# A gMLP and FFT kernel whose opening is dealt out anew among VectorE, ScalarE and GpSimd

## The chip, the cores and the metric

The kernel runs on one core of a Trainium2 chip. The metric is the device time of one execution in microseconds (us). Engines are named as in the profile: PE is TensorE's matmul (PEld its weight load), DVE is VectorE, ACT is ScalarE, POOL is GpSimd, SP is SyncE, which only issues DMAs here.

## The reference, cut to what matters

Two branches work on the same normalized input and are summed with it. The change touches the first half of branch B only, and the normalization ahead of it.

```python
xn = _layernorm(x)                               # x: 2048 x 448
return x + _A_ref(xn, w_r, w_i) + _B_ref(xn, w1, w2, w3, w4)

def _A_ref(x, w_r, w_i):                         # spectral filter
    X = rfft2(x) * (w_r + 1j * w_i)
    return irfft2(X)

def _B_ref(x, w1, w2, w3, w4):
    h = _gelu(_layernorm(x) @ w1)                # 448 x 448
    hs = concatenate(quarters of h, shifted by +1, -1, +2, -2 tokens) @ w2
    x1 = x + hs
    h2 = _gelu(_layernorm(x1) @ w3) @ w4         # 448 x 1792, 1792 x 448
    return x1 + h2
```

## The kernel before

The 2048 tokens are 16 blocks of 128. They are taken in four groups of four blocks: `GRP = [[14, 15, 0, 1], [2, 3, 4, 5], [6, 7, 8, 9], [10, 11, 12, 13]]`; two blocks share one tile `xt`. Every f32 operand of a product is split into a high and a low f16 half, and three products (high times high, high times low, low times high) replace one.

The opening does for each group, in this order: statistics of each block on VectorE (`stats`, `bn_stats` at L306 and `bn_aggr` at L307) and a first inverse root of the variance (L324 to L328); the normalization of each of the four blocks in place (`norm1`, L333 on ScalarE, L336 on VectorE or GpSimd, the engine of each block given by a list); transposes of the four blocks on TensorE (L389, `T1`); their evacuation into the f16 tile `xT`, the high half by ScalarE (L393), the low half by VectorE (L394). Then come the products with w1 (`w1_in`, L420), one unit to a block; gelu (L459) and the scaled high half (L460) on ScalarE, and the low half on VectorE in two pieces (L462). These are written into shifted slots of `x2mem`. A DMA transpose on SP's queue (L470) then makes `h` of a block, once all units that write into its slot are through. `w2_tile` (L478) multiplies an `h` block by the split w2, and L479 adds the result to the block on VectorE, scaled by `cs`. The last group takes another way: ScalarE and VectorE split it into halves (`turn`, L860 to L862) and DMA transposes (L863) turn it.

GpSimd also refines the inverse root in a run of small steps (L343 to L352), which end in `gsc`, the scale for the group's gelu, and makes `cs` for the residual (`scales`, L360 to L367).

The weights are scaled by powers of two taken from their sums of squares: ScalarE squares them (`squares`, L253), VectorE sums (L258), TensorE adds up over the partitions (L260), and VectorE makes the scale (`powers`, L262 to L267). `split_w` then splits a weight. Without an engine named for the low half, ScalarE makes the high half (L280) and VectorE the low one (L281). With GpSimd named, GpSimd first scales the weight in place (L276), ScalarE copies the high half (L277) and GpSimd subtracts (L278). Quarters 0 and 1 of w1 go the first way, 2 and 3 the second, and so do all four of w2. Two DMAs (L924, L925) then copy w2's halves to the other partitions.

The order on each engine's queue is fixed when the program is built: a scheduler sorts the instructions, bound by the written order, by priorities and by `behind(...)`, which puts an engine's instructions behind a named earlier one of that engine. It adds no wait. At run time each engine goes through its queue in order, and so does SP.

Of the kernel before, what the change touches and what calls it, by code (L numbers as in the profile page):

```python
# [125 lines left out]
def body(tc, nc, x, wf, w1, w2, w3, w4, c_g, c_n, c_small, out):  # L126
# [32 lines left out]
    pc = pool("pc")  # L159
# [8 lines left out]
    def xb(b):  # L168
        return xt[b // 2][:, b % 2]
# [103 lines left out]

    def split_w(hi, lo, src, s, low=None):
        if low is P:
            after["ps"] = (P.tensor_scalar(out=src, in0=src, scalar1=s, scalar2=0.0, op0=ALU.mult, op1=ALU.add).ins,)  # L276
            i = A.activation(out=hi, in_=src, func=AF.Copy)  # L277
            j = P.tensor_tensor(out=lo, in0=src, in1=hi, op=ALU.subtract)  # L278
            return i.ins, j.ins
        i = A.activation(out=hi, in_=src, func=AF.Copy, scale=s)  # L280
        j = V.scalar_tensor_tensor(out=lo, in0=src, scalar=s, in1=hi, op0=ALU.mult, op1=ALU.subtract)  # L281
        return i.ins, j.ins
# [16 lines left out]

    def stats(src, key, mv=None, pins=None):  # L300
        if mv is None:
            mv = pc.tile([128, 4, 2], F32, tag="mv", bufs=3, name=f"mv{key}")
        for i, s in enumerate(src):
            st = pc.tile([128, 6], F32, tag="st", bufs=4, name=f"st{key}_{i}")
            with behind(*pins[i]) if pins else contextlib.nullcontext():
                V.bn_stats(out=st, in_=s)  # L306
            V.bn_aggr(out=mv[:, i, :], in_=st)  # L307
        return mv
# [9 lines left out]

    def norm1(g, apply, pins=None):

        bs, c = GRP[g], slice(4 * g, 4 * g + 4)
        mv, a, y, nm = mva[:, c], va[:, :, c], vy[:, :, c], nma[:, c]
        stats([xb(b) for b in bs], f"a{g}", mv, pins)
        V.tensor_scalar(out=a[:, 1], in0=mv[:, :, 1], scalar1=1.0 + EPS, scalar2=EPS * EPS, op0=ALU.mult, op1=ALU.add)  # L324
# [118 lines left out]
    def wrap_on():  # L443
        move(pairs[1], pairs[0], -1)
# [442 lines left out]
    for t in range(2):  # L887
        w1_in(0, list(enumerate(first)), [t])
    n = 2
    for unit in list(enumerate(first))[:n]:  # L890
        w1_in(0, [unit], [2, 3])
# [6 lines left out]
    with behind("T", "a1"):  # L898
        for unit in list(enumerate(first))[n:2]:
            w1_in(0, [unit], [2, 3])  # L900
    with behind("n", 1), behind("u"):
        s2, r2 = powers(m2, 1, "2", first[0][:, 448:512])
    with behind("p2"):
        for unit in list(enumerate(first))[2:]:
            w1_in(0, [unit], [2, 3])
    s12 = pc.tile([128, 4], F32, name="s12")
# [9 lines left out]
    with behind("a1"), behind("n", 2):  # L916
        for k in range(2, 4):
            w1_unit(0, k, first[k])
    wrap_on()
    with behind("g", 1), behind("na", 2):  # L920
# [187 lines left out]
```

## Time and profile before

| what | value |
|---|---|
| time, median of 3 runs | 408.12 us (407.88 to 408.28) |
| the profiled execution | 408.05 us |
| its span | 406.3 us |
| mean granted TensorE clock | 0.998 |
| TensorE busy over the span | 399.9 us, 98% |
| VectorE, ScalarE, GpSimd busy | 82%, 63%, 25% |

The span is the time between the first and the last instruction of the profile; the rest of the execution's time lies around it. Rows of a timeline give the start in us, the duration of the row's instructions together, the engine, the line, the operation, the tile written and those read, the count, and in brackets the idle time ahead of the row and what ended it. A row's duration can reach past the start of the next, since instructions overlap at their ends. A row of a DMA list gives the size and the time from issue to landing.

### The profile page before, as it was taken

How to read it: one execution, taken by the hardware profiler on the slowest of the kernel's cores; microseconds unless marked ns; L12 is line 12 of the kernel's file. 1: busy time of each engine (PE TensorE's matmuls, PEld its weight loads, DVE VectorE, ACT ScalarE, POOL GpSimd, SP SyncE). 2: the span in 40 equal slices, each digit the busy share in tenths (PEclk: the TensorE clock that was granted, in tenths of full speed). 3: DMA queues.
4: the chain of work that ended last, by engine and by line, in shares of the span. 5: the costliest groups of instructions: out<-in, count | busy, mean ns of one | idle time of the engine just before them, and what ended most of it. 6: DMA issues, size and time to landing. Idle time of an engine off the chain costs nothing.

```text
span 406.3 us, 8732 instructions
## 1 busy us (share of the span) xinstructions
PE 399.9 (98%) x3391; PEld 297.2 (73%) x3391; DVE 333.6 (82%) x702; ACT 255.1 (63%) x433; POOL 100.4 (25%) x158
## 2 busy tenths in 40 slices
PE   8999999999999999999999999999999999999996
PEld 3555555865667877777878878777677779998995
DVE  5898799898947887988698888965999999965645
ACT  4788889874568857655698878853354544353431
POOL 6859910111146946500021111110000000000000
PEclk9999999999999999999999999999999999999999
DMA  8978975567489661637256556510011023100101
GB/s 280 389 272 160 249 152 138 122 121 163 95 225 266 234 191 46 219 95 185 72 144 164 162 142 161 139 27 2 24 69 70 24 90 92 47 2 2 45 2 45
DMA packets 54596, 52.07 MB, mean 128 GB/s; under 512 B 35678, under 2 KB 48542, under 8 KB 54556
## 3 DMA queue, kind: packets, MB, share of 16 engines
q1 hardware_dynamic: 54556, 51.53, 46.0%
q8 instruction: 26, 0.43, 0.4%
q14 instruction: 14, 0.11, 0.1%
HBM read 38.28 MB, written 3.67 MB: 103 GB/s over the span
## 4 chain that ended last, share of the span: by engine, by line
PE 87%; POOL 5%; DMA 2%; DVE 2%; ACT 2%; issue 1%; SPq 0%; POOLq 0%; ACTq 0%
PE pw L400 33%; PE acc L808 23%; PE pw L478 6%; PE side L778 4%; PE acc L778 3%; PE pu L667 3%; PE ps L567 3%; PE pe L688 2%; PE pp L622 2%; PE px L639 2%; PE py L709 2%; PE pw L420 2%; DMA w1s<-w 1%; POOL xt L336 1%; DMA h<-x2mem 1%
## 5 line engine op out<-in xcount | busy, mean ns | idle before, releaser
L400 PE MATMUL pw<-x2mem,w3p 128*128 128x256 f16 x1232 | 151.3, 273 | 0.0
L400 PEld LDWEIGHTS <-w3p 128*128 128x128 f16 x1232 | 118.9, 98 | 19.3
L808 PE MATMUL acc<-w4p,hf 128*128 128x448 f16 (+1 forms) x516 | 104.4, 348 | 0.0
L808 PEld LDWEIGHTS <-hf 128*128 128x128 f16 x516 | 50.1, 98 | 37.6
L726 ACT ACTIVATE pw<-pw,pe 128x512 f32<-128x512 f32 x42 | 27.4, 654 | 26.8 <-PE pw L400 26.6
L729 DVE SCALAR_TENSOR_TENSOR hf<-pw,h,hf 128x512 f16<-128x512 f32 x42 | 31.3, 746 | 12.9 <-ACT hf L728 12.7
L478 PE MATMUL pw<-w2p,h 128*128 128x448 f16 x176 | 35.8, 353 | 0.9 <-DMA h<-x2mem 0.9
L420 PE MATMUL pw<-w1p,xT 128*128 128x448 f16 x176 | 34.9, 352 | 0.1
L648 POOL TENSOR_TENSOR z<-te 128x450 f32<-128x450 f32 x16 | 15.7, 983 | 70.8 <-DVE te L646 65.9
L728 ACT ACTIVATE hf<-pw,h 128x512 f16<-128x512 f32 x42 | 28.9, 687 | 5.0 <-PE acc L808 4.0
L478 PEld LDWEIGHTS <-h 128*128 128x128 f16 x176 | 17.0, 98 | 17.0 <-DMA h<-x2mem 2.0
L744 ACT ACTIVATE hz<-g,h 128x896 f16<-128x896 f32 x14 | 14.6, 1044 | 23.1 <-DVE g L741 23.1
L420 PEld LDWEIGHTS <-xT 128*128 128x128 f16 x176 | 17.1, 99 | 16.1 <-DVE xT L394 0.4
L778 PEld LDWEIGHTS <-hz 128*128 128x128 f16 x294 | 28.3, 98 | 0.6
L629 ACT ACTIVATE pf<-pp 64x450 f16<-64x450 f32 x32 | 17.4, 544 | 12.5 <-DVE pf L630 9.7
L630 DVE TENSOR_TENSOR pf<-pp,pf 64x450 f16<-64x450 f32 x32 | 19.9, 622 | 5.1 <-ACT pf L629 4.7
L745 DVE SCALAR_TENSOR_TENSOR hz<-g,h,hz 128x896 f16<-128x896 f32 x14 | 16.1, 1148 | 6.8 <-ACT hz L744 6.8
L550 POOL TENSOR_TENSOR f<-xr 128x452 f32<-128x452 f32 x16 | 19.7, 1251 | 0.6
L558 DVE TENSOR_TENSOR xh<-f,xh 128x452 f16<-128x452 f32 x16 | 14.3, 916 | 5.7 <-ACT xh L557 5.7
L644 ACT ACTIVATE te<-px 64x450 f32<-64x450 f32 x32 | 17.3, 541 | 1.2 <-PE px L639 0.6
L738 ACT ACTIVATE g<-pw,pe 128x512 f32<-128x512 f32 x14 | 9.6, 683 | 11.3 <-PE pw L400 11.3
L547 POOL TENSOR_TENSOR xr<-xf 128x452 f32<-128x452 f32 x8 | 9.2, 1156 | 22.3 <-issue 16.4
(188 smaller groups left out, 705.7 us busy)
## 6 DMA issues: line engine op xcount, KB each, us to landing
wc<-wf SPq DMA_DIRECT2D x32, 225.0 KB, 3.7
wl<-wf SPq DMA_DIRECT2D x8, 450.0 KB, 4.3
xt<-x SPq DMA_DIRECT2D x8, 448.0 KB, 7.1
xf<-x SPq DMA_DIRECT2D x8, 448.0 KB, 4.6
loads<-x SPq DMA_DIRECT2D x7, 448.0 KB, 4.0
out<-xt SPq DMA_DIRECT2D x13, 224.0 KB, 1.9
w3raw<-w SPq DMA_DIRECT2D x3, 896.0 KB, 10.8
gn<-c_g SPq DMA_DIRECT2D x16, 128.0 KB, 3.0
```

The costliest lines, as they stand in the source:

```text
L400: T.matmul(ps_out, wp[:, wi + t, cols], xT[:, xi + t, tok], start=t == 0 and wi + xi == 0, stop=t == 3 and wi == 4)
L420: m = T.matmul(pm[:, :D], xTs[g][:, xi + t, 128 * i:128 * i + 128], w1p[:, wi + t], start=t == 0 and p == 0, stop=t == 3 and p == 2)
L478: T.matmul(pm[:, :D], h[:, k], w2p[:, w], start=n == 0, stop=n == 10)
L550: P.tensor_tensor(out=f[:, :, k:k + 2].rearrange("p b s d -> p s b d"), in0=u[:, :, 0], in1=u[:, :, 1], op=op)
L629: A.activation(out=hi, in_=src, func=AF.Copy)
L630: V.tensor_tensor(out=lo, in0=src, in1=hi, op=ALU.subtract)
L644: A.activation(out=e[64 * h:64 * h + 64], in_=px_[64 - 64 * h:128 - 64 * h, :2 * DF], func=AF.Copy)
L726: A.activation(out=pm, in_=pm, func=AF.Gelu_apprx_tanh, scale=r3)
L728: i = A.activation(out=h[:, 0], in_=pm, func=AF.Copy, scale=h3)
L729: j = V.scalar_tensor_tensor(out=h[:, 1], in0=pm, scalar=h3, in1=h[:, 0], op0=ALU.mult, op1=ALU.subtract)
L778: m = T.matmul(to, h[:, hi, 128 * blk:128 * blk + 128], b[wi], start=new and n == 0, stop=n == 2 and (last if blk in (2, 5, 3, 0) else end ...
L808: m = T.matmul(to, h[:, hi, o:o + 128], w4p[0][:, wi, f, r], start=first and f % 2 == 0 and n == 0, stop=end and f % 2 == 1 and n == 2, sk ...
```

## The change

Five things are changed.

- The first group is normalized by GpSimd, VectorE, VectorE, VectorE and no longer by GpSimd and VectorE in turn.
- The high half of w1's quarter 0 is made by GpSimd (a scaling into f16) in place of ScalarE. The low half stays on VectorE.
- The second group's fourth block gets its statistics from ScalarE: a copy with accumulation for the mean, a square with accumulation, and a small copy for the variance. The order of the other blocks' statistics is shifted, and the squares of w2 come behind ScalarE's statistics.
- w2 is scaled by GpSimd as before; its first quarter's high half is put directly behind the scalings, the second and third stay behind ScalarE's normalization of the third group, and the fourth is a copy on VectorE. All subtractions stay on GpSimd, behind its normalizations.
- The last product of each of the first two units, which needs the last low half of w1, may now stand behind both units' other products.

```diff
-    def split_w(hi, lo, src, s, low=None):
+    def split_w(hi, lo, src, s, low=None, high=None):
...
-        i = A.activation(out=hi, in_=src, func=AF.Copy, scale=s)
+        if high is P:
+            i = P.tensor_scalar(out=hi, in0=src, scalar1=s, scalar2=0.0, op0=ALU.mult, op1=ALU.add)
+        else:
+            i = A.activation(out=hi, in_=src, func=AF.Copy, scale=s)
...
-    def stats(src, key, mv=None, pins=None):
+    def stats(src, key, mv=None, pins=None, on_a=None):
...
+            if i == on_a:
+
+                sq = pc.tile([128, 1], F32, tag="sq", bufs=2, name=f"sq{key}")
+                junk = xr.bitcast(F32)[:, :D]
+                with behind(*pins[i]):
+                    A.activation(out=junk, in_=s, func=AF.Copy, scale=1.0 / D, accum_out=mv[:, i, 0:1])
+                A.activation(out=junk, in_=s, func=AF.Square, scale=-1.0, bias=mv[:, i, 0:1], accum_out=sq)
+                u = A.activation(out=mv[:, i, 1:2], in_=sq, func=AF.Copy, scale=1.0 / D)
+                after["sq"] = (u.ins,)
+                continue
...
-    n1 = [norm1(0, [P,V,P,V])]
+    n1 = [norm1(0, [P, V, V, V])]
...
-            after["w1", t] = split_w(w1p[:, t], w1p[:, 4 + t], w1s[:, t], s1, P if t > 1 else V)
+            after["w1", t] = split_w(w1p[:, t], w1p[:, 4 + t], w1s[:, t], s1, (V, V, P, P)[t], P if t in (0,) else A)
...
-    n1.append(norm1(1, [P, V, A, V], [("r1",), ("a0", 0), ("w1", 0), ("w1", 1)]))
-    with behind("w1", 3):
+    n1.append(norm1(1, [P, V, A, V], [("e1",), ("w1", 0), ("w1", 1), ("a0", 3)], 3))
+    with behind("sq"):
         squares(m2, flat(w2s))
...
+    r = [slice(0, 128)] * 3 + [slice(0, 64)]
+    with behind("g", 1):
+        for k in range(4):
+            i = P.tensor_scalar(out=w2s[r[k], k], in0=w2s[r[k], k], scalar1=s2[r[k]], scalar2=0.0, op0=ALU.mult, op1=ALU.add)
+    with behind("g", 1):
+        u = A.activation(out=w2p[r[0], 0], in_=w2s[r[0], 0], func=AF.Copy)
+    with behind("np", 2):
+        v = P.tensor_tensor(out=w2p[r[0], 7], in0=w2s[r[0], 0], in1=w2p[r[0], 0], op=ALU.subtract)
...
+    with behind("n", 2):
+        u = V.tensor_copy(out=w2p[r[3], 3], in_=w2s[r[3], 3])
+    with behind("np", 2):
+        v = P.tensor_tensor(out=w2p[r[3], 10], in0=w2s[r[3], 3], in1=w2p[r[3], 3], op=ALU.subtract)
...
     with behind("g", 1), behind("na", 2):
-        for k in range(4):
-            r = slice(0, 128 if k < 3 else 64)
-            after["w2", k] = split_w(w2p[r, k], w2p[r, 7 + k], w2s[r, k], s2[r], P)
```

The edits move instructions on the queues, also where the text is not changed. The changed kernel's lines from L284 on are numbered higher: L276 to L278 keep their numbers, L394 becomes L407, L462 becomes L475, L863 becomes L876 and so on.

GpSimd's queue at the first group, before: the normalizations of two blocks, the two scalings of w1, then the small refining steps (`vq`, from the root `vy`).

```order
L336 TENSOR_SCALAR xt_83<-xt_83,vy,nma 128x448
L336 TENSOR_SCALAR xt_76<-xt_76,vy,nma 128x448
L276 TENSOR_SCALAR w1s<-w1s,pe_205 128x448 x2
L343 TENSOR_TENSOR vq_198<-vy 128x8
L344 TENSOR_TENSOR vq_198<-vq_198,va 128x8
```

The same place in the changed kernel:

```order
L349 TENSOR_SCALAR xt_83<-xt_83,vy,nma 128x448
L281 TENSOR_SCALAR w1p<-w1s,pe_205 128x448
L276 TENSOR_SCALAR w1s<-w1s,pe_205 128x448 x2
L356 TENSOR_TENSOR vq_198<-vy 128x8
L357 TENSOR_TENSOR vq_198<-vq_198,va 128x8
```

One normalization has left, and w1's high half stands between the scale `pe` and the scalings. Everything up to the second group's normalization follows in the same order as before, but for the last low half of w1, which stands one small step earlier.

VectorE's queue at the second group's transposes, before: the sum for w2's scale (`pt`), the low halves of unit 1 (`x2mem<-pw_01`), the low half of the first transposed quarter (`xT<-pta`), the next step of w2's scale, the second quarter.

```order
L258 TENSOR_REDUCE pt_351<-m_168 128x1
L462 SCALAR_TENSOR_TENSOR x2mem<-pw_01_210,h_252,x2mem 128x2x112 x2
L394 TENSOR_TENSOR xT_322<-pta_323,xT_322 128x512
L262 TENSOR_SCALAR pt_351<-pw_00_209 128x1
L394 TENSOR_TENSOR xT_322<-pta_330,xT_322 128x512
```

The same place in the changed kernel:

```order
L258 TENSOR_REDUCE pt_352<-m_168 128x1
L407 TENSOR_TENSOR xT_323<-pta_324,xT_323 128x512
L475 SCALAR_TENSOR_TENSOR x2mem<-pw_01_210,h_252,x2mem 128x2x112 x2
L262 TENSOR_SCALAR pt_352<-pw_00_209 128x1
L407 TENSOR_TENSOR xT_323<-pta_331,xT_323 128x512
```

The first transposed quarter has moved ahead of unit 1's low halves, which now stand between it and the rest. ScalarE's queue has the same exchange for the high halves.

SP's queue after the first four h blocks, before: the rest of w3 and six parts of w4, then the transposes of the last group's halves (`xT<-x`) and of the next four h blocks (`h_598`), in turn.

```order
L223 DMA w3raw<-w 64x1792 x2
L238 DMA w4half<-w 128x6x448
L863 DMA_TRANSPOSE xT_720<-x_721 128x7x128
L470 DMA_TRANSPOSE h_598<-x2mem 128x7x128
L863 DMA_TRANSPOSE xT_720<-x_721 128x7x128 x2
L470 DMA_TRANSPOSE h_598<-x2mem 128x7x128
```

The same place in the changed kernel:

```order
L223 DMA w3raw<-w 64x1792 x2
L238 DMA w4half<-w 128x6x448
L876 DMA_TRANSPOSE xT_721<-x_722 128x7x128 x2
L483 DMA_TRANSPOSE h_599<-x2mem 128x7x128
L876 DMA_TRANSPOSE xT_721<-x_722 128x7x128 x2
L483 DMA_TRANSPOSE h_599<-x2mem 128x7x128 x3
```

Two transposes of the last group stand ahead of the first h block now, where there was one. On TensorE the products of the third group's units are dealt differently around the first two `w2_tile`s: between the first product on the first h block and the first on the second stand 23 products (11 with w2, 12 with w1) where there were 17 (11 and 6). And on GpSimd the four normalizations of the last group stand ahead of most of the steps that make `cs`, and no longer behind them.

More of the change, by code (lines that the diff above doesn't have):

```diff
@@ L888, in body @@
         w1_in(0, list(enumerate(first)), [t])
-    n = 2
-    for unit in list(enumerate(first))[:n]:
-        w1_in(0, [unit], [2, 3])
+    units = list(enumerate(first))
+    w1_in(0, [units[0]], [2, 3])
+    w1_in(0, [units[1]], [2, 3])
     with behind("ps"):
         n1[0]()
-    n1.append(norm1(1, [P, V, A, V], [("r1",), ("a0", 0), ("w1", 0), ("w1", 1)]))
-    with behind("w1", 3):
+    n1.append(norm1(1, [P, V, A, V], [("e1",), ("w1", 0), ("w1", 1), ("a0", 3)], 3))
+    with behind("sq"):
         squares(m2, flat(w2s))
     T1(1)
-    with behind("T", "a1"):
-        for unit in list(enumerate(first))[n:2]:
-            w1_in(0, [unit], [2, 3])
     with behind("n", 1), behind("u"):
@@ L903, in body @@
     with behind("p2"):
-        for unit in list(enumerate(first))[2:]:
-            w1_in(0, [unit], [2, 3])
+        w1_in(0, [units[2]], [2, 3])
+    with behind("p2"):
+        w1_in(0, [units[3]], [2, 3])
     s12 = pc.tile([128, 4], F32, name="s12")
```

16 lines of the change are left out of this document (14 added, 2 removed).

## The prediction

> **What bounds the kernel now.** I read the page's busy times first, then a table by stretches of the span, then TensorE's own timeline.
>
> ```profile
> PE 399.9 (98%) x3391; PEld 297.2 (73%) x3391; DVE 333.6 (82%) x702; ACT 255.1 (63%) x433; POOL 100.4 (25%) x158
> ```
> ```profile
> 53.00:190.00 137.00, 137.00 (x1069) 95.67 (x1068) 117.82 (x246) 95.77 (x161) 44.93 (x51) 1.00 0.62 161
> ...
> 192.00:406.00 214.00, 211.01 (x2052) 173.99 (x2050) 171.78 (x321) 118.72 (x200) 15.73 (x16) 1.00 0.25 72
> ```
> In the table the first number after the stretch is its length, the second TensorE's busy time. From 53 to 190 us TensorE never stops, and hardly after it. So whatever TensorE has lost or won when it reaches 53 us stays to the end; no later slack takes it up. The whole change lies ahead of that point.
>
> ```profile
> 9.54 0.38 PE L260 MATMUL pm<-pt,ones 128*128 128x1 f32 x2 [0.37 <-DVE pt L258]
> ...
> 11.72 6.92 PE L420 MATMUL pw<-w1p,xT 128*128 128x448 f16 x34
> 19.30 1.97 PE L389 MATMUL pta<-ident,xt 128*128 128x128 f32 x16 [0.66 <-POOL xt L336]
> 21.10 0.28 PE L260 MATMUL pw<-pt,ones 128*128 128x1 f32 x2
> 21.24 10.37 PE L420 MATMUL pw<-w1p,xT 128*128 128x448 f16 x54
> 31.45 1.91 PE L389 MATMUL pta<-ident,xt 128*128 128x128 f32 x16
> 33.72 1.31 PE L478 MATMUL pw<-w2p,h 128*128 128x448 f16 x6 [0.36 <-DMA h<-x2mem]
> ...
> 36.00 1.11 PE L478 MATMUL pw<-w2p,h 128*128 128x448 f16 x5
> 37.39 2.26 PE L478 MATMUL pw<-w2p,h 128*128 128x448 f16 x11 [0.28 <-DMA h<-x2mem]
> ...
> 46.67 4.33 PE L478 MATMUL pw<-w2p,h 128*128 128x448 f16 x22
> 51.21 1.12 PE L478 MATMUL pw<-w2p,h 128*128 128x448 f16 x5 [0.22 <-DMA h<-x2mem]
> ```
> Here is what there is to win. The 54 products take 10.37 us, 0.19 each; the last one's record runs 0.16 past the moment at which the next could start, so a true pause is the printed idle time plus 0.16. The pauses: 0.8 us before the second group's transposes at 19.30 (waiting for GpSimd's normalization); 0.5 at 33.72, 0.44 at 37.39 and 0.38 at 51.21, all three for a DMA transpose of h. That is 2.1 us together.
>
> **Term A: the second group's transposes (19.30).** They need all four blocks, and GpSimd's comes last.
>
> ```profile
> 10.82 1.25 POOL L276 TENSOR_SCALAR w1s<-w1s,pe 128x448 f32<-128x448 f32 x2 [0.83 <-DMA w1s<-w]
> ...
> 14.07 0.73 POOL L348 TENSOR_TENSOR vz<-vw 128x8 f32<-128x8 f32 x1
> 14.88 0.20 POOL L349 TENSOR_TENSOR vz<-vz,vq 128x8 f32<-128x8 f32 x1
> ...
> 16.45 1.03 POOL L278 TENSOR_TENSOR w1p<-w1s,w1p 128x448 f16<-128x448 f32 x1
> ...
> 18.30 0.94 POOL L336 TENSOR_SCALAR xt<-xt,vy,nma 128x448 f32<-128x448 f32 x1
> ```
> ```profile
> 10.06 0.18 DVE L307 BATCH_NORM_AGGREGATE mva<-sta 128x2 f32<-128x6 f32 x1
> 10.15 0.13 DVE L262 TENSOR_SCALAR pt<-pm 128x1 f32<-128x1 f32 x1
> ...
> 14.09 0.66 DVE L281 SCALAR_TENSOR_TENSOR w1p<-w1s,pe,w1p 128x448 f16<-128x448 f32 x1
> ...
> 16.92 0.58 DVE L324 TENSOR_SCALAR va<-mva 128x4 f32<-128x4 f32 x1
> 17.42 0.16 DVE L325 TENSOR_SCALAR va<-mva 128x4 f32<-128x4 f32 x1
> ...
> 18.22 1.26 DVE L336 TENSOR_SCALAR xt<-xt,vy,nma 128x448 f32<-128x448 f32 x2
> ```
> GpSimd works without a pause from 10.82 to 18.30. Taking one block of the first group off it ahead of that wins nothing, because at 10.82 it waits for the scale of w1. What the change adds is one operation inside this row of work, the first quarter of w1's high half. The f32 scalings cost 1.25 / 2 = 0.62 each; the subtraction, which also writes f16, 1.03. I take 0.62 (one input, like the scalings) and keep 1.0 as the far end. The scale itself comes 0.15 earlier, since a block's statistics no longer stand between TensorE's sum (done 9.54 + 0.38 = 9.92) and the step at 10.15. So GpSimd reaches its block at 18.30 + 0.62 - 0.15 = 18.77.
>
> VectorE, relieved of one block's statistics (0.53 at its spacing) and of waiting, starts the closing steps of the statistics at about 16.2 and its two normalizations at about 17.1, an estimate from the rows above. That helps VectorE and ScalarE, but neither is last. And it moves VectorE's normalizations onto GpSimd's last split and small steps. A step that costs 0.20 alone (14.88) took 0.73 beside VectorE's split (14.09), so an overlap costs GpSimd up to 0.5; I take 0.2. Its block then runs alone, 0.72 for 0.94, which gives 0.22 back. Sum: 0.62 - 0.15 + 0.2 - 0.22 = 0.45, rounded to **+0.5 us**; ends -0.2 (one of the overlaps with the w1 splits missed) and +1.1 (1.0 for the new operation, 0.5 for the overlap).
>
> The Trainium skill, page "SBUF — State Buffer", section on SBUF's two separate sides, says that the port pair shared by VectorE and GpSimd is an exclusive lock, held for a whole instruction. The 0.58 us at 16.92, against 0.16 for its twin, beside GpSimd's split from 16.45 to 17.48, agrees with it. By that rule both normalizations would lock GpSimd out for their whole length, and A would be near its upper end.
>
> ScalarE's two passes and a copy for the fourth block cost about 0.58 + 0.20 twice and 0.2, by its rows on 448 columns:
>
> ```profile
> 16.09 0.20 ACT L253 ACTIVATION_READ_ACCUMULATOR xr<-w2s 128x1 f32 x1
> 18.22 0.76 ACT L333 ACTIVATE xt<-xt,nma,vy 128x448 f32<-128x448 f32 x1 [1.93 <-DVE nma L328]
> ```
> They are hidden by the 1.93 us in which it waited; without that cover they would cost about 1.7. I cost them at nothing.
>
> **Term B: VectorE behind the transposes.** VectorE now evacuates the first transposed quarter before the two low halves of unit 1, and not after them.
>
> ```profile
> 20.24 0.81 DVE L462 SCALAR_TENSOR_TENSOR x2mem<-pw,h,x2mem 128x224 f16<-128x224 f32 x2 [0.70 <-POOL vw L346]
> 20.97 0.68 DVE L394 TENSOR_TENSOR xT<-pta,xT 128x512 f16<-128x512 f32 x1
> ...
> 27.91 0.81 DVE L462 SCALAR_TENSOR_TENSOR x2mem<-pw,h,x2mem 128x224 f16<-128x224 f32 x2 [0.19 <-ACT x2mem L460]
> ```
> Before, the 0.73 us of those two (spacing 20.24 to 20.97) lay in a hole while the transposes ran. Now the quarter starts some 0.3 sooner after the transposes and the two follow: about 0.4 of later work. The 0.19 idle at 27.91 swallows part. The low halves that complete the first h block, its transpose, and so TensorE's pause at 33.72 move by **+0.25** (ends 0 and 0.4).
>
> **Term C: from the first h transpose to 51.21.** Two things here. On TensorE, 23 products instead of 17 now stand between the first and second h blocks: 33.72 + 23 x 0.19 = 38.1, later than the 37.39 at which the second block released TensorE. The pause of 0.44 goes. ScalarE has two copies fewer ahead of the group's evacuation, so the operands are there. But on SP the second transpose for xT now stands ahead of the first h transpose of the next four blocks, which TensorE needs at 51.21.
>
> ```profile
> 37.80 1.22 SPq L223 DMA_DIRECT2D w3raw<-w  x2
> 39.07 0.59 SPq L238 DMA_DIRECT2D w4half<-w  x1
> 44.65 1.82 SPq L863 DMA_TRANSPOSE xT<-x  x1
> 46.57 1.83 SPq L470 DMA_TRANSPOSE h<-x2mem  x1
> ```
> ```profile
> w4half<-w SPq DMA_DIRECT2D x1, 1344.0 KB, 10.6
> ...
> xT<-x SPq DMA_TRANSPOSE x1, 5.8
> ...
> h<-x2mem SPq DMA_TRANSPOSE x1, 4.6
> xT<-x SPq DMA_TRANSPOSE x1, 3.5
> ```
> The second fence gives the time from issue to landing of each (the last for the one issued at 48.51). The w4 load lands at 39.07 + 10.6 = 49.6, the transposes at 44.65 + 5.8 = 50.4, 46.57 + 4.6 = 51.2 and 48.51 + 3.5 = 52.0. They come out in the order of issue, the first just behind the load and the others 0.8 apart, whatever the issue time. So the transposes queue behind the load. Issuing them about a microsecond earlier, which the changed order on GpSimd and ScalarE allows, wins nothing; one more ahead costs 0.8: the h block lands at 52.0. Slightly earlier loads may give 0 to 0.4 back; I take 0.1. **C = +0.7** for the arrival at 53 us, and it includes the 0.44 just won, since TensorE only waits longer at this gate. GpSimd's scales for the first h block also come some 0.5 to 1.0 later, behind the last group's normalizations, which may stop TensorE at 46.7; the gate swallows that too.
>
> The w2 edits otherwise move cover, not the path: GpSimd's scalings stay where they were, one copy goes to VectorE, and the subtractions end within about 0.2 of before.
>
> **Sum.** 0.5 + 0.25 + 0.7 = 1.45 us on the profiled execution, 408.05 (span 406.3 and 1.75 around it), which stands 0.07 under the median of 408.12: **409.5 us**.
>
> **Rivals.**
> 1. *No extra transpose at the gate.* The h block still lands where it did, because the load ends 0.8 sooner. Then C is 0 and the sum 0.75: 408.8. For it: the load's issue stands behind three h transposes that may flow more smoothly. Against: the 0.8 spacing. Chance 0.15.
> 2. *The lock at full length.* VectorE's two normalizations (1.26 us as they ran) block GpSimd wholly: A = 1.1 and the sum about 2.1, 410.1. It is the rule named above; the 0.73 against 0.20 speaks for it, the 0.94 against 0.72 where they overlapped in full speaks against. Chance 0.13.
> 3. *Faster: the transposes do not queue behind the load.* The mechanism is the gate at 51.21. If h lands by issue time (46.57 + about 3), both 0.44 and 0.38 vanish, C = -0.8, and with A and B near zero the time is 407.2. It decides once the h block lands before 50.4 in the old clock. Against it: 5.8, 4.6 and 3.5, which shrink as the load drains. Chance 0.07.
> 4. *All terms at their small ends*: A 0, B 0, C 0.4, 408.5. Chance 0.07.
>
> **How the numbers follow.** The forecast has 0.58. About 0.2% (0.8 us) is what a measurement here can tell from no change, so slower means over 408.9 and faster under 407.3. Slower: the forecast and rival 2, 0.71, say 0.70. Within: rivals 1 and 4, 0.22. Faster: 0.08. The range runs from the ends near A -0.2, B 0, C 0.3 (408.2) to A 1.1, B 0.4, C 0.8 (410.4).
>
> **What would show it.** A: the second group's transposes start near 19.8, released by GpSimd, with VectorE's normalizations done by about 18. If they start before 19.3, A is wrong. B: the first w2 products come about 2.5 to 2.8 after those of the third group's transposes begin, against 33.72 - 31.45 = 2.27 before. C: no pause before the second h block; one of a microsecond or more before the fifth, released by a DMA transpose that lands 0.8 after the one ahead of it and 2.4 after the w4 load. If that load lands well before 49.6 or the transposes pass it, C is wrong and with it the sign.

## The result, and the profile after

The changed kernel takes 410.18 us (median of 4 runs, 409.88 to 410.42) against 408.00 of the kernel before beside it (407.84 to 408.28): a ratio of 1.0049, 95% interval 1.0037 to 1.0061. It is slower by 2.1 us. Ratios here and below are of fast runs; a single execution of the w2 edits alone that took 1493.08 us is in none of them. The forecast was 409.5, the range 408.2 to 410.4. The profiled execution took 410.19 us with a span of 408.3, 2.0 more than before.

TensorE's timeline of the changed kernel, the rows that answer to those of before (start and duration in us, idle time and its releaser in brackets; 0.16 is to be added to the idle time for the true pause, as in the prediction):

```profile
9.81 0.34 PE L260 MATMUL pm<-pt,ones 128*128 128x1 f32 x2
...
11.79 6.59 PE L433 MATMUL pw<-w1p,xT 128*128 128x448 f16 x34
19.57 1.97 PE L402 MATMUL pta<-ident,xt 128*128 128x128 f32 x16 [1.18 <-POOL xt L349]
...
31.73 1.47 PE L402 MATMUL pta<-ident,xt 128*128 128x128 f32 x12
33.56 0.63 PE L402 MATMUL pta<-ident,xt 128*64 128x128 f32 x4 [0.36 <-DVE x2mem L475]
34.43 1.12 PE L491 MATMUL pw<-w2p,h 128*128 128x448 f16 x5 [0.24 <-DMA h<-x2mem]
...
38.79 2.25 PE L491 MATMUL pw<-w2p,h 128*128 128x448 f16 x11
...
47.87 4.32 PE L491 MATMUL pw<-w2p,h 128*128 128x448 f16 x22 [0.78 <-DVE xt L492]
52.55 2.25 PE L491 MATMUL pw<-w2p,h 128*128 128x448 f16 x11 [0.36 <-DMA h<-x2mem]
...
146.38 0.83 PE L580 MATMUL ps<-csm,xh 128*128 128x128 f16 x12 [0.49 <-DVE y L585]
```

Of the old pauses, the one of 0.5 us ahead of the first w2 product is now two, 0.52 inside the third group's transposes (33.56) and 0.40 behind them (34.43); the second h block (38.79) no longer waits. That at the second group's transposes reads longer (1.18 for 0.66 idle), but only because TensorE has fewer small pauses ahead of it. New are 0.94 at 47.87, where VectorE's addition frees a bank for TensorE's results late, and 0.65 at 146.38, long after the front. Set beside the rows of before, the delay grows at these places:

| TensorE begins | before | after | late by |
|---|---|---|---|
| the sum for w1's scale | 9.54 | 9.81 | 0.27 |
| the second group's transposes | 19.30 | 19.57 | 0.27 |
| the third group's transposes | 31.45 | 31.73 | 0.28 |
| the first w2 product | 33.72 | 34.43 | 0.71 |
| the products of the fifth h block | 51.21 | 52.55 | 1.34 |
| the first FFT product | 131.64 | 133.03 | 1.39 |
| end of the span | 406.3 | 408.3 | 2.0 |

So there are four losses: 0.27 ahead of everything, nothing at the second group's transposes, 0.43 up to the first w2 product, 0.63 up to the fifth h block, and 0.6 after the first FFT product. The table by stretches confirms the last one (the length, then TensorE's busy time): it never stops from 54 to 143 us and then loses half a microsecond.

```profile
54.00:143.00 89.00, 89.00 (x630) 59.28 (x628) 75.27 (x183) 62.95 (x106) 25.46 (x34) 1.00 0.71 165
143.00:148.00 5.00, 4.50 (x45) 3.26 (x44) 4.75 (x6) 2.89 (x6) 4.92 (x4) 1.00 0.39 112
```

In the prediction's terms the profiled execution gives: the opening 0.27 for 0, A 0.0 for 0.5, B 0.43 for 0.25, C 0.63 for 0.7, and about 0.65 that no term covers.

### The profile page after: what moved, and what is told of

Read it like the earlier page. It is cut to its first block, busy times and chain, and to the rows that moved or that the text cites. A ratio compares the mean times of both kernels' runs of the same rounds, so it can differ in the third digit from the quotient of the medians.

```text
span 408.3 us, 8740 instructions
## 1 busy us (share of the span) xinstructions
PE 400.4 (98%) x3391; PEld 297.6 (73%) x3391; DVE 334.3 (82%) x702; ACT 255.1 (62%) x436; POOL 100.1 (25%) x158
## 4 chain that ended last, share of the span: by engine, by line
PE 63%; ACT 3%; POOL 1%; DVE 1%; issue 1%; POOLq 0%
PE pw L413 25%; PE acc L821 17%; PE side L791 4%; PE acc L791 3%; PE pu L680 3%; PE pe L701 2%; PE pp L635 2%; PE px L652 2%; PE py L722 2%; PE ps L580 2%; POOL f L563 1%; ACT xf L554 1%; ACT xh L570 1%; ACT pw L739 1%; ACT hf L741 0%
## 5 line engine op out<-in xcount | busy, mean ns | idle before, releaser
L742 DVE SCALAR_TENSOR_TENSOR hf<-pw,h,hf 128x512 f16<-128x512 f32 x42 | 31.2, 744 | 13.8 <-ACT hf L741 13.5
L491 PEld LDWEIGHTS <-h 128*128 128x128 f16 x176 | 17.1, 98 | 17.1 <-DMA h<-x2mem 1.3
L570 ACT ACTIVATE xh<-f 128x452 f16<-128x452 f32 x16 | 8.7, 573 | 10.6 <-POOL f L563 8.9
```

Of the source, the lines that this page charges most:

```text
L491: T.matmul(pm[:, :D], h[:, k], w2p[:, w], start=n == 0, stop=n == 10)
L742: j = V.scalar_tensor_tensor(out=h[:, 1], in0=pm, scalar=h3, in1=h[:, 0], op0=ALU.mult, op1=ALU.subtract)
```

## The experiments

Theory: B is VectorE's order at the second group's transposes; C is the order of the transposes behind the w4 load; the last 0.65 us come from the changed order on ScalarE and VectorE near 100 us, which delays the fold ahead of the FFT (sums and differences that GpSimd makes of the FFT's input, `xr` and `f`). Rivals: everything is lost at the front; the copy of w2 on VectorE, held up by GpSimd, is the cause of B; the late pause has nothing to do with order. Runs of one front differ in where the sum for w1's scale begins: 9.35, 9.54, 10.08 and 10.14 us in four profiled executions whose code is that of the kernel before up to there, by when the first loads land. So places are compared from that sum, or from the second group's transposes on. The kernel before took 408.0 to 408.1 beside each group of runs.

**The w2 copy back on ScalarE.**

```diff
-    with behind("n", 2):
-        u = V.tensor_copy(out=w2p[r[3], 3], in_=w2s[r[3], 3])
+    with behind("na", 2):
+        u = A.activation(out=w2p[r[3], 3], in_=w2s[r[3], 3], func=AF.Copy)
```

> The changed kernel, with the last quarter of w2's high half copied by ScalarE again and no longer by VectorE. My theory: that copy lasted 1.18 us on VectorE, because GpSimd's subtraction of w2 beside it held it up, and it pushed the low halves of the second group; so without it the new pause of 0.53 us inside the third group's transposes goes, and the first h block lands about 0.4 us sooner against the third group's transposes. How much of that reaches the end depends on GpSimd's scales cs (pause of 0.94 us at 46.7): if they come as before, that pause grows by what was won. I expect 0.4 to 1.0 us less than the changed kernel's 410.2: 409.2 to 409.8. Rival (the copy is only cover, as the prediction had it): the pause inside the transposes stays and the time is 410.2.

409.26 us (409.12 to 409.44, 6 runs), ratio 1.0031 (1.0019 to 1.0042). First the row in question, in the changed kernel, on VectorE and on GpSimd:

```profile
31.61 1.18 DVE L951 CAST w2p<-w2s 64x448 f16<-64x448 f32 x1
```
```profile
31.51 1.03 POOL L938 TENSOR_TENSOR w2p<-w2s,w2p 128x448 f16<-128x448 f32 x1
```

The copy begins 0.10 after the subtraction and ends 0.25 after it. The rule of the Trainium skill, page "SBUF — State Buffer", section on its two separate sides, by which the engine that comes second is blocked for the whole instruction of the first, agrees. TensorE without that copy:

```profile
31.97 1.91 PE L402 MATMUL pta<-ident,xt 128*128 128x128 f32 x16
34.66 1.31 PE L491 MATMUL pw<-w2p,h 128*128 128x448 f16 x6 [0.78 <-DMA h<-x2mem]
```

The pause inside the transposes is gone, and the first w2 product comes no sooner: 2.69 us after the start of these transposes, 2.70 with the copy. The wait for the h block is simply whole again (0.78 + 0.16 for 0.52 + 0.40). So the copy is not the cause of B. The 0.9 us that the run did win came later, with an order of GpSimd's small steps that the edit changed too: GpSimd's scales were ready before TensorE needed the third bank, and no pause stood in the FFT. A pause of 0.67 stayed at the fifth h block (52.26), now released by VectorE's addition. The time was as expected, the reason was not.

**The first group dealt out as before.**

```diff
-    n1 = [norm1(0, [P, V, V, V])]
+    n1 = [norm1(0, [P, V, P, V])]
```

> The changed kernel with the first group's normalizations dealt out as in the kernel before (GpSimd, VectorE, GpSimd, VectorE); one instruction changes its engine and no other moves. My theory: VectorE's third normalization ended late (0.75 us beside GpSimd's), so the sum for w1's scale and the first group's transposes came 0.22 us later; undoing it brings the first transposes from 10.01 back to 9.79, the second group's from 19.57 to about 19.35, and the end about 0.2 us forward: 410.0. Rival (the prediction: taking the block off GpSimd costs nothing): first transposes unchanged against the changed kernel, 410.2. A third possibility: GpSimd is late with its two blocks, and then the second group's transposes do not come earlier.

409.89 us (409.73 to 410.66), ratio 1.0049 (1.0036 to 1.0063): not to be told from the changed kernel. The profiled execution was granted a clock of 0.71 from 10 to 12 us and 0.50 up to 13.4, so it isn't read past the opening. Up to there it shows that GpSimd is through with its two blocks at 10.47, 0.35 before the scale is there, so the third possibility is out. The traces of the changed kernel tell more. VectorE, and what ScalarE had done by then:

```profile
8.05 1.60 DVE L349 TENSOR_SCALAR xt<-xt,vy,nma 128x448 f32<-128x448 f32 x3
9.57 0.14 DVE L258 TENSOR_REDUCE pt<-m 128x1 f32<-128x4 f32 x1
```
```profile
8.79 0.18 ACT L253 ACTIVATION_READ_ACCUMULATOR xr<-w1s 64x1 f32 x1
```

The sum of the squares could have begun at 8.97 and began at 9.57, behind VectorE's third normalization. In another execution of the same front the sum began at 9.33, 0.03 after the last square, since there the weights had landed later. So that normalization costs 0 to 0.57, an estimate from these two executions, by when the loads land. Its mean cost wasn't measured.

**The fifth h block ahead on SP.**

```diff
-            d = SY.dma_start_transpose(out=xTs[g][:, :, 128 * i:128 * i + 128], in_=h)
+            with behind("h", 2, 0) if i else contextlib.nullcontext():
+                d = SY.dma_start_transpose(out=xTs[g][:, :, 128 * i:128 * i + 128], in_=h)
```

> The changed kernel with the DMA transpose of the fifth h block put on SP's queue ahead of the second one for xT; the other engines' queues stay, but for some products on TensorE that trade places. My theory (term C): the transposes come out in the order of issue, 0.77 us apart, behind the w4 load; so the h block lands about 0.77 us sooner, near 51.7, the pause of 0.52 us at 51.84 goes, and the time falls by 0.5 to 409.7. Rival: the order on the queue does not matter, the block lands near 52.5, and the time stays 410.2.

410.19 us (410.02 to 410.96), ratio 1.0057 (1.0045 to 1.0070): no gain at all, though the gate, the wait ahead of the fifth h block, opened as expected. TensorE there and at the FFT:

```profile
47.65 6.49 PE L491 MATMUL pw<-w2p,h 128*128 128x448 f16 x33 [0.80 <-DVE xt L492]
```
```profile
144.96 0.83 PE L580 MATMUL ps<-csm,xh 128*128 128x128 f16 x12 [0.16 <-DVE y L585]
146.37 0.83 PE L580 MATMUL ps<-csm,xh 128*128 128x128 f16 x12 [0.58 <-DVE y L585]
```

33 products stand in one piece: no pause at 51.8. The step of the FFT that waits begins at 146.37, where it began in the changed kernel (146.38). What the front won, a wait 95 us later took back. But the fold had begun 0.42 us sooner (119.87 for 120.29). It lost that in its second part, on GpSimd beside VectorE, whose addition had waited for a load:

```profile
126.98 1.15 DVE L533 SCALAR_TENSOR_TENSOR xt<-xt,s,loads 128x896 f32<-128x896 f32 x1 [0.55 <-DMA loads<-x]
```
```profile
127.71 1.35 POOL L560 TENSOR_TENSOR xr<-xf 128x452 f32<-128x452 f32 x1 [3.76 <-issue]
129.01 1.93 POOL L561 TENSOR_TENSOR xr<-xf 128x452 f32<-128x452 f32 x1
```

In the changed kernel these two steps took 1.06 each, from 128.13; the third part begins at 133.03 in both. So the locally right term was worth nothing in this order. The late wait is not a fixed bound: here it is a sooner start and longer steps. That the other executions lost the gain in the same way isn't shown.

**The last mean subtractions on GpSimd.**

```diff
-    ln2(range(12, 16), [P, A, P, A], ("f", 0, 6))
+    ln2(range(12, 16), [P, P, P, P], ("f", 0, 6))
```

> The changed kernel with the four mean subtractions of the last four blocks of the second normalization all on GpSimd, where two were on ScalarE; nothing else moves. My theory: the last 0.66 us were lost at 145.7, where TensorE waited for the folded input of the FFT, because VectorE gave the last blocks' statistics 3 us later than before, and ScalarE's in-order queue held the gelu behind its mean subtractions. Without those on ScalarE the gelu at 115 comes 1 to 3 us sooner, the fold follows, the pause of 0.66 us goes or shrinks to under 0.2, and the time is 409.5 to 409.8. Rival (all is lost at the front and the pause at 145.7 has another cause): 410.2, with the pause as it was.

410.29 us, ratio 1.0059 (1.0046 to 1.0071). The pause at 145 shrank only from 0.66 to 0.52. ScalarE's gelu did come 3.0 us sooner (112.11 for 115.07), but then ScalarE waited:

```profile
116.00 2.35 ACT L522 ACTIVATE y<-y,vs 128x448 f16<-128x448 f32 x4 [2.50 <-DVE vs L301]
```

VectorE's last statistics ended at 112.1 to 112.2 in both kernels, and its small steps up to `vs` at 115.91, half a microsecond later than in the changed kernel (115.42): beside GpSimd's mean subtractions four of them took 0.40 to 0.58, where 0.16 is usual. So freeing ScalarE's queue at that place is not enough, since the way through VectorE's statistics is as long. How much the queue alone would cost, this run can't tell.

**Two subtractions back in their place.**

```diff
                 if e is A:
-                    A.activation(out=o[-1][:, i], in_=xb(b0 + m + i), func=AF.Identity, bias=c)
+                    with behind("f", 0, 3) if b0 == 8 else contextlib.nullcontext():
+                        A.activation(out=o[-1][:, i], in_=xb(b0 + m + i), func=AF.Identity, bias=c)
```

> The changed kernel with two instructions moved on ScalarE: the mean subtractions of blocks 9 and 11 ahead of the second MLP half stand behind the high half of product pair 3, where they stood in the kernel before (VectorE's queue shifts a few steps with them). My theory of the last 0.66 us: the scheduler had put these two ahead of that high half, they wait for statistics, VectorE stands idle 3.4 us at 99.6 behind the high half, gives the last statistics at 112 (108 before), and the fold of the FFT, paced by GpSimd from there on, is late at 145.7. So with the order restored VectorE's wait falls to 1 or 2 us, the fold's first step (120.3) comes at least 1 us sooner, the pause at 145.7 goes, and the time is 409.5. Rival (the fold is late for another reason): the pause stays and the time is 410.2.

409.46 us (409.26 to 409.53), ratio 1.0033 (1.0021 to 1.0046): 0.7 less, as expected. The rows of the chain, in the changed kernel first: VectorE behind the high half, GpSimd's first step of the fold.

```profile
103.07 0.75 DVE L742 SCALAR_TENSOR_TENSOR hf<-pw,h,hf 128x512 f16<-128x512 f32 x1 [3.43 <-ACT hf L741]
```
```profile
120.29 1.06 POOL L560 TENSOR_TENSOR xr<-xf 128x452 f32<-128x452 f32 x1 [5.07 <-ACT xf L555]
```

The same two, and TensorE at the FFT, with the subtractions in their place:

```profile
99.49 0.75 DVE L743 SCALAR_TENSOR_TENSOR hf<-pw,h,hf 128x512 f16<-128x512 f32 x1 [0.34 <-ACT hf L742]
```
```profile
117.59 1.06 POOL L561 TENSOR_TENSOR xr<-xf 128x452 f32<-128x452 f32 x1 [5.07 <-ACT xf L556]
```
```profile
144.76 1.50 PE L581 MATMUL ps<-csm,xh 128*128 128x128 f16 x24
```

VectorE's wait falls from 3.43 to 0.34, the fold begins 2.7 us sooner, and the 24 products of the FFT stand in one piece. So the order on ScalarE at 100 us, with the few steps of VectorE that shift with it, is enough to make or remove the changed kernel's loss after 143 us. That it is the only way to lose there isn't shown; the front edits alone, below, lose there without it.

**Both together.** The edit is that of the last run and that of the fifth h block.

> Both edits: the fifth h block's transpose ahead of the second for xT, and the two mean subtractions back in their place. In the run with the first alone the pause at 51.8 went, but the pauses from 125 to 146 grew from 0.66 to 1.35 us and the time stayed. My theory: two separate losses, of which the later hides the earlier, so together they give back 0.5 + 0.66: 409.0. Rival 1 (the fold's pace is a floor set elsewhere, by GpSimd): 409.5, as the second alone. Rival 2 (neither is a loss): 410.2.

409.09 us, ratio 1.0021 (1.0005 to 1.0037). The two add up: 0.7 for the fold (410.18 to 409.46) and 0.4 more for the gate. The intervals of the two times overlap, but the traces agree: TensorE is through with the fifth h block 44.41 us after the sum for w1's scale, against 44.77 with the fold's edit alone, and neither pauses in the FFT. The gain at the gate shows as soon as the fold no longer hides it.

**The same gate in the kernel before.**

```diff
-            d = SY.dma_start_transpose(out=xTs[g][:, :, 128 * i:128 * i + 128], in_=h)
+            with behind("h", 2, 0):
+                d = SY.dma_start_transpose(out=xTs[g][:, :, 128 * i:128 * i + 128], in_=h)
```

> The kernel before, with one swap on SP's queue and nothing else: the fifth h block's transpose ahead of the first for xT. My theory (term C): transposes leave in the order of issue, 0.77 us apart, behind the w4 load; so this block lands at 50.4 in place of 51.2, the pause of 0.38 us at 50.64 goes, and the time falls by 0.4 to 407.7, if nothing later takes it back. Rival: landing is set by the time of issue and not by the order; the block lands near 51.2 again, 408.1. Another: the last group's products now wait for xT, and the time rises.

408.05 us, ratio 1.0000 (0.9991 to 1.0009): not the gain that was expected. The block's transpose was issued at 45.47 and landed 5.5 us later, 0.8 after the w4 load and ahead of xT, as the theory has it. But TensorE still waited:

```profile
51.73 2.24 PE L478 MATMUL pw<-w2p,h 128*128 128x448 f16 x11 [0.18 <-DVE xt L479]
```
```profile
51.01 0.67 DVE L479 SCALAR_TENSOR_TENSOR xt<-xt,cs,pw 128x448 f32<-128x448 f32 x1
```

The releaser has changed from the DMA to VectorE, whose addition frees the bank at 51.68. The gate had a second door right behind the first, which the profile of before could not name, because a wait is put down to the condition that came last.

**w1's high half back on ScalarE.**

```diff
-            after["w1", t] = split_w(w1p[:, t], w1p[:, 4 + t], w1s[:, t], s1, (V, V, P, P)[t], P if t in (0,) else A)
+            after["w1", t] = split_w(w1p[:, t], w1p[:, 4 + t], w1s[:, t], s1, (V, V, P, P)[t], A)
```

> The changed kernel with the high half of w1's first quarter on ScalarE again. My theory of term A: the operation cost GpSimd 0.64 us, but the change gave GpSimd about as much back (the small refining steps are no longer held up twice by VectorE's low halves, and the scale comes earlier), so that the second group's transposes came no later. Taking the 0.64 away should then bring GpSimd's block and the second group's transposes 0.3 to 0.6 us forward, counted from the sum for w1's scale (9.76 us in the changed kernel), and the time to 409.6 to 410.0. Rival (GpSimd's block is not what sets those transposes, or ScalarE's copy now sets w1's products): no change there, 410.2.

409.25 us (409.11 to 409.54), ratio 1.0030 (1.0018 to 1.0041). Less than expected in time and for another reason: the second group's transposes came 9.65 us after the sum for w1's scale, only 0.1 sooner than in the changed kernel (9.76), although GpSimd had 0.64 us less to do. VectorE and GpSimd there:

```profile
16.84 1.01 DVE L337 TENSOR_SCALAR va<-mva 128x4 f32<-128x4 f32 x1
```
```profile
18.43 0.20 POOL L356 TENSOR_TENSOR vq<-vy 128x8 f32<-128x8 f32 x1 [0.32 <-DVE vy L340]
18.66 0.94 POOL L349 TENSOR_SCALAR xt<-xt,vy,nma 128x448 f32<-128x448 f32 x1
```

GpSimd now waits for VectorE's small steps, one of which was held up for some 0.85 (1.01, against 0.16 for its twin) while GpSimd ran its second subtraction. The two engines arrive together, so relief of either one alone brings little. The rest of the 0.9 is a balance of waits that moved: 0.51 and not 0.94 before the third w2 bank, no pause at the fifth h block nor at the FFT, but new ones of 0.37 at 56.4 and 0.59 at 81.2.

**The statistics back on VectorE.**

```diff
-    n1.append(norm1(1, [P, V, A, V], [("e1",), ("w1", 0), ("w1", 1), ("a0", 3)], 3))
-    with behind("sq"):
+    n1.append(norm1(1, [P, V, A, V], [("r1",), ("a0", 0), ("w1", 0), ("w1", 1)]))
+    with behind("w1", 3):
         squares(m2, flat(w2s))
```

> The changed kernel with all of the second group's statistics on VectorE again and the squares of w2 in their old place. VectorE's order at the second group's transposes becomes the old one with it (unit 1's low halves ahead of the first quarter of xT); the orders further on stay those of the changed kernel. My theory of term B: that order is the cause, so the first w2 product comes about 0.45 us sooner, counted from the sum for w1's scale (24.6 in the changed kernel, 24.2 before), the w4 load and with it the gate about 0.3 sooner, and the late loss stays: 409.8 to 410.0. The statistics themselves cost nothing either way, since GpSimd's block ends last. Rival (ScalarE's part was what relieved VectorE and made up for the rest): second group's transposes 0.3 to 0.5 later and the time above 410.4.

409.59 us (409.42 to 409.78), ratio 1.0039 (1.0027 to 1.0051). GpSimd and TensorE:

```profile
18.94 0.20 POOL L356 TENSOR_TENSOR vq<-vy 128x8 f32<-128x8 f32 x1 [0.33 <-DVE vy L340]
```
```profile
20.16 1.97 PE L402 MATMUL pta<-ident,xt 128*128 128x128 f32 x16 [0.52 <-POOL xt L349]
...
34.53 1.12 PE L491 MATMUL pw<-w2p,h 128*128 128x448 f16 x5 [0.25 <-DMA h<-x2mem]
```

Both theories were half right. From the second group's transposes to the first w2 product it takes 34.53 - 20.16 = 14.37 us, as before (33.72 - 19.30 = 14.42) and not as in the changed kernel (34.43 - 19.57 = 14.86). In all 14 profiled executions this stretch goes with the order at the second group's transposes: 14.37 to 14.43 us in the five with the old one, 14.85 to 14.94 in the nine with the new one, whatever else differs. So term B is that order. ScalarE's exchange of the high halves goes with VectorE's in every one, so the two engines' parts can't be told apart. But the transposes themselves came 10.27 after the sum for w1's scale and no longer 9.76: GpSimd waited for VectorE, which had the fourth block's statistics to do and one low half of w1 held up (1.41 for 0.67) beside GpSimd's subtraction. So beside the other edits ScalarE's statistics, costed at nothing, win 0.5 us at this place, and the new order gives it back. The time is below both expectations, since less was lost at the fold (0.24).

**The w2 edits alone, and the front edits alone.** The first run is the kernel before with the new code for w2, the second the changed kernel with the old loop for w2.

> The kernel before with the w2 edits alone. On SP the second transpose for xT stands ahead of the fifth h block's, and on ScalarE the two mean subtractions ahead of product pair 3's high half, both as in the changed kernel; VectorE's order at the second group's transposes is the old one. My theory: these edits, which the prediction called cover, carry the gate and the late loss. The first h block lands as in the kernel before (24.2 us after the sum for w1's scale), no pause before the second; the fifth lands 0.8 us later than before, and the fold of the FFT is late as in the changed kernel. Sum 0.6 to 0.8 for the gate and 0.4 to 0.7 for the fold: 409.1 to 409.6. Rival (the w2 edits only move cover): 408.1.

> The changed kernel with the old code for w2, so the front edits alone (first group's list, w1's high half, statistics on ScalarE). SP's and ScalarE's orders are those of the kernel before, VectorE's at the second group's transposes is that of the changed kernel. My theory: what is left is term B (0.45 us at the first h block) and VectorE's third normalization (0 to 0.5 us ahead of the sum for w1's scale); the gate at 51 us passes on about 0.3 of B, since the w4 load is issued behind the h transposes; no late loss. 408.4 to 408.9. Rival (the loss is all at the front): near 410.2. With the run of the w2 edits alone, the two parts should add up to the whole 2.1 us within 0.4.

408.92 us, ratio 1.0019 (1.0010 to 1.0028), and 409.08 us, ratio 1.0025 (1.0015 to 1.0036). The two losses, 0.9 and 1.0, add up to 1.9 of the 2.1 us. The w2 edits alone show both the late scales and the wider gate on TensorE:

```profile
46.81 4.32 PE L478 MATMUL pw<-w2p,h 128*128 128x448 f16 x22 [0.78 <-DVE xt L479]
51.58 2.25 PE L478 MATMUL pw<-w2p,h 128*128 128x448 f16 x11 [0.45 <-DMA h<-x2mem]
```

Here 51.58 is 42.23 after the sum for w1's scale, 0.56 more than before: term C without the front. From there to the end this execution lost nothing more, and no pause stood at the fold, against my expectation. The front edits alone lost 0.44 there, also against it, with ScalarE's old order:

```profile
145.29 0.83 PE L580 MATMUL ps<-csm,xh 128*128 128x128 f16 x12 [0.28 <-DVE y L585]
```

In that run ScalarE's last mean subtraction waited for a DMA transpose of `y`, and began 1.87 later than before (111.52), while the first FFT product came only 0.52 later:

```profile
113.39 0.67 ACT L512 ACTIVATE y<-xt,nm 128x448 f32<-128x448 f32 x1 [2.29 <-DMA x2mem<-y]
```

What decides in most runs is how far GpSimd's first fold step lies ahead of TensorE's first FFT product:

| run | first fold step | first FFT product | between | pause near 145 |
|---|---|---|---|---|
| changed kernel | 120.29 | 133.03 | 12.74 | 0.66 |
| fifth h block ahead on SP | 119.87 | 132.62 | 12.75 | 1.06 |
| last subtractions on GpSimd | 119.97 | 132.87 | 12.90 | 0.52 |
| first group dealt out as before | 120.86 | 133.75 | 12.89 | 0.52 |
| front edits alone | 119.18 | 132.16 | 12.98 | 0.44 |
| statistics on VectorE | 119.99 | 133.17 | 13.18 | 0.24 |
| w2 edits alone | 118.61 | 132.01 | 13.40 | none |
| w2 copy on ScalarE | 118.44 | 132.68 | 14.24 | none |
| kernel before | 117.32 | 131.64 | 14.32 | none |
| two subtractions in place | 117.59 | 132.73 | 15.14 | none |

Distance and pause together make 13.4 in five of the six runs here that pause; the sixth, with the fifth h block ahead on SP, makes 13.8, by the longer steps shown above. The kernel before had 0.9 us to spare, which its profile doesn't show as a wait anywhere. The w2 edits alone use all of it up (13.40) without a pause.

**An attempt to beat both.** The kernel before with the h block first on SP, the subtractions behind the high half, and on VectorE the addition ahead of a unit's low halves:

```diff
-    for k in range(4):
+    w1_unit(2, 0)
+    for b in range(3):
+        w2_tile(b)
+    for k in range(1, 4):
         w1_unit(2, k)
...
-            v = V.scalar_tensor_tensor(out=h[1][:, k], in0=pv_[:, k], scalar=h1, in1=h[0][:, k],
+            with behind("acc", 2) if (g, i) == (2, 1) else contextlib.nullcontext():
+                v = V.scalar_tensor_tensor(out=h[1][:, k], in0=pv_[:, k], scalar=h1, in1=h[0][:, k],
```

> An attempt to beat both kernels, from the kernel before. In the run with the h block ahead of xT's transposes the block landed 0.8 us sooner and the pause at the gate stayed at 0.34, now behind VectorE's addition of the third w2 result, which frees the bank. Here that addition also stands ahead of unit 21's low halves on VectorE, and the two mean subtractions stay behind product pair 3's high half (the scheduler shifts more behind 60 us). My theory: the gate has these two doors, so with both open the pause of 0.38 us goes: 407.7. Rival: a third door (GpSimd's scales, or a bank) holds the gate, or the shifted order loses later what is won: 408.0 to 408.8.

407.98 us (407.58 to 410.38, 11 runs), ratio 1.0007 (0.9996 to 1.0018): no gain that can be measured. The gate is open, in TensorE's row of all 33 products:

```profile
46.79 6.41 PE L479 MATMUL pw<-w2p,h 128*128 128x448 f16 x33
```

In the profiled execution it is 378.4 us from the second group's transposes to TensorE's last row of products (19.57 to 397.97), against 379.0 before (19.30 to 398.28), but the runs don't bear that out. Part of it is hidden in this execution by its opening: the sum for w1's scale began 0.54 later than in the profile of before (10.08 for 9.54). Whether the other executions opened late too is open.

## Why the prediction was right, and where it was not

The direction and the range were right, partly by luck: up to 53 us errors of opposite sign nearly cancel (1.34 for 1.45), and then comes a loss of 0.65 that no term had. The measured 410.18 lies nearest to the 410.1 of rival 2, whose mechanism (A at 1.1) did not occur: A was nothing.

- **"Taking one block of the first group off it ... wins nothing."** Nothing is won, but what VectorE gets for it can cost: 0 to 0.57 ahead of the sum for w1's scale, 0.27 between the two profiled executions. The step counted GpSimd's relief and not VectorE's load.
- **Term A** was mis-sized: 0.0 for 0.5. The rows of GpSimd in the changed kernel:

```profile
10.83 0.64 POOL L281 TENSOR_SCALAR w1p<-w1s,pe 128x448 f16<-128x448 f32 x1 [1.42 <-DVE pe L267]
11.44 1.69 POOL L276 TENSOR_SCALAR w1s<-w1s,pe 128x448 f32<-128x448 f32 x2
13.10 0.20 POOL L356 TENSOR_TENSOR vq<-vy 128x8 f32<-128x8 f32 x1
13.37 0.20 POOL L357 TENSOR_TENSOR vq<-vq,va 128x8 f32<-128x8 f32 x1
...
14.01 0.47 POOL L359 TENSOR_TENSOR vw<-vw,vq 128x8 f32<-128x8 f32 x1
...
14.89 0.20 POOL L361 TENSOR_TENSOR vz<-vw 128x8 f32<-128x8 f32 x1
...
18.56 0.95 POOL L349 TENSOR_SCALAR xt<-xt,vy,nma 128x448 f32<-128x448 f32 x1
```

  The operation itself took 0.64, as estimated (0.62). But the hold-ups beside VectorE changed places: the scalings 1.69 for 1.25 and one step 0.47 for 0.20, while the steps of 0.70 and 0.73 took 0.20 each. That is -0.32 net, and the scale came 0.26 sooner against the sum (0.15 was forecast): 0.64 - 0.32 - 0.26 = 0.06. The block begins 8.75 us after the sum for w1's scale, where it was 8.76. The sign given for A (19.8, wrong under 19.3) goes by the span's clock, and there the late opening hid the miss (19.57). The terms "+0.2" and "-0.22" failed: the overlaps that vanish were not counted, and the block kept its 0.95. The full lock of rival 2 shows in single rows (the copy above) but did not add up at this place.
- **"That helps VectorE and ScalarE, but neither is last"** failed. In the kernel before, the `vy` that GpSimd's step ahead of its block needs was ready 0.08 us before that step began:

```profile
17.82 0.17 DVE L327 TENSOR_SCALAR vy<-vy 128x8 int32<-128x8 int32 x1
```
```profile
18.07 0.20 POOL L343 TENSOR_TENSOR vq<-vy 128x8 f32<-128x8 f32 x1
```

  In the runs with w1's high half or the statistics put back GpSimd waited 0.32 and 0.33 for VectorE. They were tied, and the statistics on ScalarE pay for the new operation on GpSimd. VectorE's two normalizations came at 17.99, not at the forecast 17.1, since one closing step, begun at 16.65, took 0.62 beside GpSimd's subtraction.
- **Term B** had the right mechanism, 0.43 for 0.25, and its sign came (2.70 us, forecast 2.5 to 2.8). The idle time that was to swallow part of it did not; one step beside GpSimd's scalings took 0.56, where it had taken 0.22.
- **Term C** was right in mechanism and size, 0.63 for 0.7. The rows of SP, and the times from issue to landing:

```profile
39.75 0.59 SPq L238 DMA_DIRECT2D w4half<-w  x1
43.84 5.11 SPq L876 DMA_TRANSPOSE xT<-x  x2
49.05 1.49 SPq L483 DMA_TRANSPOSE h<-x2mem  x1
```
```profile
w4half<-w SPq DMA_DIRECT2D x1, 1344.0 KB, 10.4
...
h<-x2mem SPq DMA_TRANSPOSE x1, 3.5
```

  The load lands at 50.15 and the block at 52.5, 2.4 later: three transposes 0.8 apart. The pause of 0.44 went, the scales came late (0.94 at 47.87), and the gate swallowed both, as forecast; so the pause left at the gate was 0.52, and not the microsecond or more of the sign. The Trainium skill, page "DMA: Bandwidth & Descriptors", section on queues, rings and completion order, says that each DMA engine takes a ring's descriptors in order. The landings here come in the order of issue, which agrees.
- **"Whatever TensorE has lost or won when it reaches 53 us stays to the end ... The whole change lies ahead of that point"** is the step that failed most. The edits lie ahead of 53 us, but the scheduler dealt out the queues anew as far as 112 us, and the fold had 0.9 us of slack that no pause showed. Part of it is "the w2 edits otherwise move cover, not the path": alone they cost 0.9 us, in their profile no more than term C, but the cover they used up is the fold's slack (14.32 to 13.40), and with the front edits beside them that is a loss.

Open: why the transpose of `y` that holds up the fold is late with the front edits alone, where ScalarE's order is the old one; the mean cost of the first group's list; what the fifth edit, the last products of the first two units, is worth by itself; and why the open gate of the last attempt doesn't show in the time.

## What to carry to other kernels

A pause that vanishes from a profile is not yet time won: ask which second condition stood just behind the first (the bank behind the DMA, VectorE behind GpSimd), and whether a later wait, here 95 us on, takes the gain back. Where a scheduler orders the whole program, read its order as far as it differs, not as far as the edit reaches, and note how much slack each chain has that TensorE will need later. Between two engines that are tied at a join, moving work from one to the other changes little.

## What the runs showed of the hardware

The opening of one and the same front varied by 0.8 us between executions (the sum for w1's scale at 9.35 to 10.14), by when the weights land. A small VectorE step of 0.16 us took up to 1.01 beside a GpSimd subtraction of 1.04 (with w1's high half back on ScalarE). SP's issue of a transpose, 1.25 us in a quiet queue, took up to 2.7 while the w4 load was in flight (with the fifth h block ahead).
